# Where the low parts of split weights are subtracted: 45 subtractions move from GpSimd to VectorE

## The chip, the cores and the metric

The kernel runs on one core of a Trainium2 chip. The metric is the device time of one execution in microseconds, as the median of several runs. Beside it stands one execution that was recorded by the hardware profiler, with its own time.

## The reference

Three layers follow each other on a batch of 4 sequences of 576 tokens. All matrix products are wanted at the accuracy of float32.

```python
# attention, 8 heads of 64, over a window of 64 earlier keys
attn = softmax(where(mask, q @ k.T / 8, -1e9)) ; x = attn @ v        # (4, 576, 512)
# gated layer with a spatial product over the tokens
h = relu(x @ w_in)                                                   # 512 -> 1024
u, vv = h[..., :512], h[..., 512:]
vn = (vv - mean) / sqrt(var + 1e-6)
x = (u * (w_spatial @ vn + b_spatial)) @ w_out                       # 512 -> 512
# mixer
u = x + (relu(x.T @ w_tok1) @ w_tok2).T                              # 576 -> 256 -> 576
out = u + relu(u @ w_ch1) @ w_ch2                                    # 512 -> 1536 -> 512
```

The weights come as 64-bit floats; w_tok1 and w_tok2 are called the token weights here, w_ch1 and w_ch2 the channel weights.

## The kernel before

Every product outside the attention is made of three matmuls in a 32-bit format with fewer digits (float32r): an operand x is split into a high part hi, which is x rounded to that format, and a low part lo = x - hi; `mm3` then adds up hi*hi, hi*lo and lo*hi in PSUM. So each operand needs a cast (on ScalarE) and a subtraction (on VectorE or GpSimd) before TensorE can use it.

The work comes in stages. Until about 255 us the kernel does the attention, in 18 iterations, with the first products of the gated layer between them (`uv_u`, `uv_v`) and its product over the tokens (`spatial`); w_in, w_spatial and w_out are loaded by `load_split`. None of that is touched. The order on TensorE and on the DMA queue of SP is written out by hand in the iterations; after them, and on the other engines throughout, a planner, which simulates the instructions with costs of its own, puts each engine's instructions in order when the kernel is built. Each engine then runs its own queue strictly in that order.

After the iterations come, in the order of the program text:

- The token weights: five calls of `load_wide` (tiles t_h and t_l), through the pool lw.
- `wout(b)` for each of four batches: the gated product U (line 386) is split into gh and gl, four pieces of 128x576 each, in five buffers for gh and five for gl; then four by two groups of 12 matmuls, whose results ScalarE copies back into U (line 396).
- `x2nat(b)`: transposes of U on TensorE (line 407), and the split of the result into nh and nl (line 257). `tok1(b)` and `tok2(b)` are the two token products; tok1 splits its result into hh and hl (line 420), tok2 adds to U (line 431).
- The channel weights: w_ch1 in twelve blocks c1 (c1h, c1l) and w_ch2 in twelve blocks c2 (c2h, c2l), each one call of `load_wide` of 128x512. Blocks c1 0 to 3 are loaded beside wout; the pool p3 for the next ones opens when wout is done, and the pool c2p, for c2 3 to 11 and c1 7 to 11, opens when tok2(3) is done, since it takes the room of earlier tiles.
- The channel products over six chunks of 384 tokens: `ch1` (into the tile mm) gives g3h (line 486) and g3l (line 487, VectorE), and `ch2` (line 497, into the tile A) adds up over twelve blocks. In the first chunk of tokens the blocks are still being loaded.

One call of `load_wide` handles one chunk of a weight: a DMA into wraw (three buffers), ScalarE's absolute value into wval (line 106, two buffers), four VectorE instructions that build the 32-bit float (lines 107, 109, 110 and 111), ScalarE's cast to the high part (line 112), and the subtraction for the low part (line 113), which also frees the buffer of wval for the chunk after next. In the rows "wval" is the 32-bit float, and each line number names the same step.

In `spatial`, VectorE adds the bias to a product in PSUM (line 301, tile tmp) and multiplies U by it (line 302); three PSUM tiles of the pool psmm go round among all the mm products, so TensorE waits when line 301 is late.

Of the kernel before, what the change touches and what calls it, by code (L numbers as in the profile page):

```python
# [13 lines left out]
ALU = mybir.AluOpType  # L14
# [13 lines left out]
def f(ap):  # L28
    return ap.bitcast(F32)
# [3 lines left out]
def tile_kernel(ctx, tc, qT, kT, kE, v, w_in, wsT, b_sp, w_out, w_t1, w_t2, w_c1, w_c2, mask, outT):  # L33

    nc = tc.nc
# [57 lines left out]
    def load_wide(pl, hi, lo, src, rows=P, dup=False, wmax=S):  # L93

        shape = list(src.shape[1:])
        n = shape[0] * (shape[1] if len(shape) > 1 else 1)
        raw = pl.tile([P, 2 * wmax], F32, tag="wraw", name="wraw", bufs=3).bitcast(I32)[:, :2 * n]
        val = pl.tile([P, wmax], F32, tag="wval", name="wval", bufs=2)
        for r0 in (0, 64) if dup else (0,):
            dst = raw[r0:r0 + rows]  # L100
            nc.sync.dma_start(out=dst.rearrange("p (a c) -> p a c", a=shape[0]) if len(shape) > 1 else dst, in_=src.bitcast(I32))
        tot = P if dup else rows
        r3 = raw.rearrange("p (n w) -> p n w", w=2)
        low, high = r3[:tot, :, 0], r3[:tot, :, 1]
        x = val[:tot, :n]
        nc.scalar.activation(out=x, in_=f(high), func=AF.Abs)
        nc.vector.tensor_scalar(out=x, in0=x, scalar1=TINY, scalar2=None, op0=ALU.max)  # L107
        xi = x.bitcast(I32)
        nc.vector.tensor_scalar(out=xi, in0=xi, scalar1=0x07FFFFFF, scalar2=3, op0=ALU.bitwise_and, op1=ALU.logical_shift_left)  # L109
        nc.vector.scalar_tensor_tensor(out=xi, in0=high, scalar=-0x40000000, in1=xi, op0=ALU.bitwise_and, op1=ALU.bitwise_or)  # L110
        nc.vector.scalar_tensor_tensor(out=xi, in0=low, scalar=29, in1=xi, op0=ALU.logical_shift_right, op1=ALU.bitwise_or)  # L111
        nc.scalar.copy(out=hi, in_=x)  # L112
        nc.gpsimd.tensor_tensor(out=lo, in0=x, in1=f(hi), op=ALU.subtract)  # L113

    def mm3(o, steps, tail=()):

        todo = []
        for sh, sl, mh, ml in steps:
            todo += [(sh, mh), (sh, ml), (sl, mh)]
        todo += tail  # L120
        n = len(todo)
        for i, (a, c) in enumerate(todo):
            nc.tensor.matmul(o, a, c, start=(i == 0), stop=(i == n - 1))  # L123
# [250 lines left out]
    for k in (0, 2):  # L374
        load_wide(lw, t1_h[:, k:k + 2, :].rearrange("p k c -> p (k c)"), t1_l[:, k:k + 2, :].rearrange("p k c -> p (k c)"),
                  w_t1[128 * k:128 * k + 256, :].rearrange("(k p) c -> p k c", p=P))
    load_wide(lw, t1_h[:, 4, :], t1_l[:, 4, :], w_t1[512:, :], rows=64, dup=True)
    for k in range(2):
        load_wide(lw, t2_h[:, k, :], t2_l[:, k, :], w_t2[128 * k:128 * k + 128, :])

    def wout(b):
        gt = []
        for d in range(4):
            gh = gp.tile([P, S], F32R, tag="gh", name="gh", bufs=5)
            gl = gp.tile([P, S], F32R, tag="gl", name="gl", bufs=5)
            us = U[:, d, b * S:b * S + S]
            nc.scalar.copy(out=gh, in_=us)
            nc.gpsimd.tensor_tensor(out=gl, in0=us, in1=f(gh), op=ALU.subtract)  # L388
            gt.append((gh, gl))
        for d in range(4):  # L390
            dc = slice(128 * d, 128 * d + 128)
            for c0 in (0, 288):
                cs = slice(c0, c0 + 288)
                ps = psmm.tile([P, 512], F32, tag="mm", name="mm")
                mm3(ps[:, :288], [(wo_h[:, k, dc], wo_l[:, k, dc], gt[k][0][:, cs], gt[k][1][:, cs]) for k in range(4)])
                nc.scalar.copy(out=U[:, d, b * S + c0:b * S + c0 + 288], in_=ps[:, :288])
# [45 lines left out]
    def load_c2(pl, k):  # L442
        c2[k] = [pl.tile([P, DM], F32R, name=f"c2{x}{k}") for x in "hl"]
        load_wide(lw, *c2[k], w_c2[128 * k:128 * k + 128, :], wmax=wmax)

    wout(0)
    run_work(len(work))
    ws_stack.close()
    c1p = pool("c1p", "left", stack=c_stack, bufs=1)
    hp = pool("hp", "left", stack=c_stack, bufs=1)  # L450
    x2nat(0)
    wout(1)
    tok1(0)
    load_c1(c1p, 0)
    x2nat(1)
    wout(2)
    tok2(0)
    load_c1(c1p, 1)
# [135 lines left out]
```

## Time and profile before

| what | value |
|---|---|
| median of 3 runs | 702.94 us (702.53 to 703.41) |
| the profiled execution | 704.92 us |
| its span in the profile | 703.1 us |
| busy: TensorE, VectorE, ScalarE, GpSimd | 657.1, 347.8, 252.6, 129.6 us |
| granted clock of TensorE, mean | 0.982 |

In what follows PE is TensorE (PEld its weight loads), DVE is VectorE, ACT is ScalarE, POOL is GpSimd and SP the engine that issues the DMAs. A busy share is an average over stages. A matmul's end is modelled, so that a PE that is shown as busy is not always at its full pace. The names "out<-in" are the program's tiles.

### The profile page before, as it was taken

How to read it: one execution, taken by the hardware profiler on the slowest of the kernel's cores; microseconds unless marked ns; L12 is line 12 of the kernel's file. 1: busy time of each engine (PE TensorE's matmuls, PEld its weight loads, DVE VectorE, ACT ScalarE, POOL GpSimd, SP SyncE). 2: the span in 40 equal slices, each digit the busy share in tenths (PEclk: the TensorE clock that was granted, in tenths of full speed). 3: DMA queues.
4: the chain of work that ended last, by engine and by line, in shares of the span. 5: the costliest groups of instructions: out<-in, count | busy, mean ns of one | idle time of the engine just before them, and what ended most of it. 6: DMA issues, size and time to landing. Idle time of an engine off the chain costs nothing.

```text
span 703.1 us, 11915 instructions
## 1 busy us (share of the span) xinstructions
PE 657.1 (93%) x4744; PEld 627.7 (89%) x4744; DVE 347.8 (49%) x912; ACT 252.6 (36%) x675; POOL 129.6 (18%) x134
## 2 busy tenths in 40 slices
PE   2398899999999998899999998999999999999997
PEld 2387799899989898799998996999999999999996
DVE  4977576645574589921369689701311312212112
ACT  3667672553664353642345154301211111111110
POOL 2534410101220173632012143300000000000000
PEclk8589999999999999999999999999999999999999
DMA  8626552322240034100042234100100100100001
GB/s 287 199 78 186 182 170 69 116 90 68 84 151 2 1 104 129 60 1 1 1 150 91 89 121 150 45 1 1 46 1 0 46 1 1 46 0 13 34 1 45
DMA packets 27286, 50.24 MB, mean 71 GB/s; under 512 B 2784, under 2 KB 13408, under 8 KB 27232
## 3 DMA queue, kind: packets, MB, share of 16 engines
q1 hardware_dynamic: 27232, 49.49, 22.2%
q8 instruction: 37, 0.61, 0.4%
q14 instruction: 17, 0.14, 0.1%
HBM read 44.76 MB, written 4.72 MB: 70 GB/s over the span
## 4 chain that ended last, share of the span: by engine, by line
PE 75%; DVE 11%; DMA 6%; ACT 3%; issue 2%; POOL 1%; SPq 1%; DVEq 0%; POOLq 0%; ACTq 0%
PE mm L123 44%; PE A L497 20%; PE sc L184 3%; DVE wval L110 3%; PE A L123 3%; DMA kk<-in_kT 2%; PE xo L225 2%; DVE wval L111 2%; PE pt L213 2%; ACT pb L199 2%; DVE wval L107 1%; DMA raw<-in_wsT 1%; DMA U<-in_w_in 1%; DVE wval L109 1%; SPq L157 1%
## 5 line engine op out<-in xcount | busy, mean ns | idle before, releaser
L487 DVE SCALAR_TENSOR_TENSOR g3l<-mm,g3h 128x384 fp32r<-128x384 f32 x72 | 40.0, 557 | 191.0 <-ACT g3h L486 191.0
L486 ACT ACTIVATE g3h<-mm 128x384 fp32r<-128x384 f32 x72 | 35.3, 493 | 220.2 <-PE mm L123 220.1
L123 PE MATMUL mm<-uh,c1h 128*128 128x384 f32 x288 | 97.0, 337 | 1.2 <-ACT c1h L112 1.2
L497 PE MATMUL A<-g3h,c2l 128*128 128x384 f32 x288 | 97.2, 338 | 0.8 <-POOL c2l L113 0.8
L123 PE MATMUL mm<-uh,c1l 128*128 128x384 f32 x288 | 96.8, 337 | 1.2 <-POOL c1l L113 1.2
L123 PE MATMUL mm<-ul,c1h 128*128 128x384 f32 x288 | 96.7, 336 | 0.0
L497 PE MATMUL A<-g3l,c2h 128*128 128x384 f32 x288 | 94.1, 337 | 0.0
L497 PE MATMUL A<-g3h,c2h 128*128 128x384 f32 x288 | 93.7, 338 | 0.0
L199 ACT ACTIVATE pb<-pb,nm 128x128 f32<-128x128 f32 x144 | 55.9, 391 | 16.8 <-DVE nm L197 13.9
L184 PE MATMUL sc<-kk,QZ 128*64 128x128 f32 x576 | 39.7, 297 | 22.5 <-DMA kk<-in_kT 16.3
L184 PEld LDWEIGHTS sc<-kk,QZ 128*64 128x64 f32 x576 | 35.8, 152 | 23.2 <-issue 21.6
L123 PEld LDWEIGHTS mm<-uh,c1h 128*128 128x128 f32 x288 | 54.0, 188 | 1.9 <-ACT c1h L112 1.9
L123 PEld LDWEIGHTS mm<-uh,c1l 128*128 128x128 f32 x288 | 54.0, 188 | 1.9 <-POOL c1l L113 1.9
L497 PEld LDWEIGHTS A<-g3h,c2l 128*128 128x128 f32 x288 | 54.0, 187 | 1.5 <-POOL c2l L113 1.4
L497 PEld LDWEIGHTS A<-g3h,c2h 128*128 128x128 f32 x288 | 53.6, 187 | 0.6 <-ACT c2h L112 0.5
L123 PEld LDWEIGHTS mm<-ul,c1h 128*128 128x128 f32 x288 | 54.0, 188 | 0.0
L497 PEld LDWEIGHTS A<-g3l,c2h 128*128 128x128 f32 x288 | 53.8, 188 | 0.0
L123 PE MATMUL mm<-ws_h,nh 128*128 128x288 f32 x160 | 47.3, 300 | 1.9 <-DVE tmp L301 1.7
L123 PE MATMUL mm<-ws_l,nh 128*128 128x288 f32 x160 | 46.5, 295 | 0.0
L123 PE MATMUL mm<-gh,wo_h 128*128 128x288 f32 x128 | 38.2, 301 | 1.0 <-DVE tmp L301 0.8
L123 PE MATMUL mm<-gl,wo_h 128*128 128x288 f32 x128 | 38.1, 298 | 0.6 <-POOL gl L388 0.4
L194 DVE CUSTOM_DVE_ANT_0 pb<-sc,msk 128x128 f32<-128x128 f32 x144 | 33.4, 283 | 9.3 <-PE sc L184 9.3
(111 smaller groups left out, 1433.0 us busy)
## 6 DMA issues: line engine op xcount, KB each, us to landing
wraw<-in_w_c SPq DMA_DIRECT2D x24, 512.0 KB, 3.5
kk<-in_kT SPq DMA_DIRECT2D x16, 384.0 KB, 4.2
QZ<-in_qT SPq DMA_DIRECT2D x36, 128.0 KB, 4.1
va<-in_v SPq DMA_DIRECT2D x18, 256.0 KB, 3.1
vb<-in_v SPq DMA_DIRECT2D x18, 256.0 KB, 4.0
outT<-ot SPq DMA_DIRECT2D x24, 192.0 KB, 2.0
U<-in_w_in SPq DMA_DIRECT2D x8, 512.0 KB, 5.6
raw<-in_w_out SPq DMA_DIRECT2D x8, 256.0 KB, 3.6
```

What stands on the lines that cost most here:

```text
L107: nc.vector.tensor_scalar(out=x, in0=x, scalar1=TINY, scalar2=None, op0=ALU.max)
L110: nc.vector.scalar_tensor_tensor(out=xi, in0=high, scalar=-0x40000000, in1=xi, op0=ALU.bitwise_and, op1=ALU.bitwise_or)
L111: nc.vector.scalar_tensor_tensor(out=xi, in0=low, scalar=29, in1=xi, op0=ALU.logical_shift_right, op1=ALU.bitwise_or)
L123: nc.tensor.matmul(o, a, c, start=(i == 0), stop=(i == n - 1))
L184: nc.tensor.matmul(sc[64 * q:64 * q + 64, h, :], qz[:, h % 2, j, 64 * q:64 * q + 64], kk[:, j, step * q:step * q + 128], start=True, stop= ...
L194: nc.vector.tensor_tensor_reduce(out=half[:, h, :], in0=scs[g][:, h, :], in1=mk, scale=1.0, scalar=-3e38, op0=ALU.add, op1=ALU.max, accum_ ...
L199: nc.scalar.activation(out=half[:, h, :], in_=half[:, h, :], func=AF.Exp, scale=SCALE, bias=nm[:, h:h + 1], accum_out=sm[:, h:h + 1])
L213: nc.tensor.transpose(pt[:, h, :], pb[:, 4 * g + h, :], ident)
L225: nc.tensor.matmul(xo[64 * e:64 * e + 64, j, 64 * q:64 * q + 64], vt[q][:, hc], PT[:, 2 * j + e, 64 * q:64 * q + 64], start=True, stop=True)
L486: nc.scalar.activation(out=gh, in_=ps[:, :CW], func=AF.Relu)
L487: nc.vector.scalar_tensor_tensor(out=gl, in0=ps[:, :CW], scalar=0.0, in1=f(gh), op0=ALU.max, op1=ALU.subtract)
L497: nc.tensor.matmul(acc[d][:, :CW], a, c, start=(ft == 0 and i == 0), stop=(ft == 11 and i == 2))
```

## The change

Two subtractions are issued to VectorE where they were issued to GpSimd: the low part of a chunk in `load_wide`, which serves the token and channel weights, and the low part gl of the gated input in `wout`. The arithmetic is the same. The subtraction in `load_split` (w_in, w_spatial, w_out itself) stays on GpSimd.

```diff
@@ load_wide
         nc.scalar.copy(out=hi, in_=x)
-        nc.gpsimd.tensor_tensor(out=lo, in0=x, in1=f(hi), op=ALU.subtract)
+        nc.vector.tensor_tensor(out=lo, in0=x, in1=f(hi), op=ALU.subtract)
@@ wout
             nc.scalar.copy(out=gh, in_=us)
-            nc.gpsimd.tensor_tensor(out=gl, in0=us, in1=f(gh), op=ALU.subtract)
+            nc.vector.tensor_tensor(out=gl, in0=us, in1=f(gh), op=ALU.subtract)
             gt.append((gh, gl))
```

## Rows read from the trace of the kernel before

**Rows 1.** The page, part 1: busy time, share of the span, instructions of each engine.

```profile
PE 657.1 (93%) x4744; PEld 627.7 (89%) x4744; DVE 347.8 (49%) x912; ACT 252.6 (36%) x675; POOL 129.6 (18%) x134
```

**Rows 2.** Windows: stretch, its length, busy us (instructions) of each engine, granted clock, DMA.

```profile
255.00:285.00 30.00, 27.35 (x200) 26.22 (x199) 28.19 (x43) 12.54 (x24) 16.13 (x12) 1.00 0.43 137
285.00:300.00 15.00, 11.59 (x70) 9.57 (x70) 14.76 (x15) 9.54 (x19) 11.61 (x8) 1.00 0.10 34
300.00:320.00 20.00, 20.00 (x144) 19.30 (x144) 4.60 (x8) 9.27 (x19) 5.78 (x5) 1.00 0.01 1
370.00:390.00 20.00, 18.76 (x111) 17.14 (x110) 19.60 (x34) 8.79 (x17) 5.56 (x4) 1.00 0.33 106
420.00:440.00 20.00, 16.76 (x87) 14.38 (x86) 19.55 (x28) 9.12 (x15) 7.19 (x6) 1.00 0.50 157
465.00:600.00 135.00, 135.00 (x771) 135.00 (x770) 28.60 (x47) 19.83 (x35) 0.00 (x0) 1.00 0.04 14
```

**Rows 3.** Groups of GpSimd: line, operation, tiles, count | busy us, mean ns.

```profile
L388 POOL TENSOR_TENSOR gl<-U,gh 128x576 fp32r<-128x576 f32 x16 | 24.5, 1563 | 20.4 <-ACT gh L387 20.4
...
L113 POOL TENSOR_TENSOR c2l<-wval,c2h 128x512 fp32r<-128x512 f32 x12 | 17.4, 1450 | 36.7 <-ACT c2h L112 36.7
L113 POOL TENSOR_TENSOR c1l<-wval,c1h 128x512 fp32r<-128x512 f32 x12 | 17.0, 1420 | 59.5 <-ACT c1h L112 59.5
...
L113 POOL TENSOR_TENSOR t_l<-wval,t_h 128x512 fp32r<-128x512 f32 (+2 forms) x5 | 7.1, 1419 | 11.8 <-ACT t_h L112 11.8
```

**Rows 4.** Timeline 254 to 266 us: start, duration, engine, line, tiles.

```profile
255.59 7.82 POOL L388 TENSOR_TENSOR gl<-U,gh 128x576 fp32r<-128x576 f32 x5
...
258.87 1.69 DVE L302 TENSOR_TENSOR U<-tmp,U 128x288 f32<-128x288 f32 x1
...
262.06 1.63 DVE L107 TENSOR_SCALAR wval<-wval 128x512 f32<-128x512 f32 x1
...
264.22 0.45 DVE L301 TENSOR_TENSOR tmp<-mm,bb 128x288 f32<-128x288 f32 x1
...
264.72 0.40 PE L123 MATMUL mm<-ws_h,nh 128*128 128x288 f32 x1 [1.72 <-DVE tmp L301]
```

**Rows 5.** Timeline 285 to 298 us.

```profile
287.79 1.74 DVE L110 SCALAR_TENSOR_TENSOR wval<-wraw,wval 128x512 int32<-128x512 int32 x1
...
294.53 1.79 DVE L110 SCALAR_TENSOR_TENSOR wval<-wraw,wval 128x512 int32<-128x512 int32 x1
...
296.24 1.28 DVE L257 TENSOR_TENSOR nl<-A,nh 128x512 fp32r<-128x512 f32 x2
...
296.97 0.50 PE L123 MATMUL A<-nh,t_h 128*128 128x512 f32 x1 [1.65 <-DVE nl L257]
```

**Rows 6.** Timeline 426 to 434 us, two chunks of the last loads.

```profile
426.41 1.28 POOL L113 TENSOR_TENSOR c2l<-wval,c2h 128x512 fp32r<-128x512 f32 x1 [2.00 <-ACT c2h L112]
...
426.51 1.73 DVE L110 SCALAR_TENSOR_TENSOR wval<-wraw,wval 128x512 int32<-128x512 int32 x1
...
428.63 0.68 DVE L111 SCALAR_TENSOR_TENSOR wval<-wraw,wval 128x512 int32<-128x512 int32 x1
429.23 0.41 DVE L107 TENSOR_SCALAR wval<-wval 128x512 f32<-128x512 f32 x1
429.34 0.62 ACT L112 CAST c1h<-wval 128x512 fp32r<-128x512 f32 x1 [0.94 <-DVE wval L111]
...
430.14 1.72 DVE L110 SCALAR_TENSOR_TENSOR wval<-wraw,wval 128x512 int32<-128x512 int32 x1
...
433.42 1.73 DVE L110 SCALAR_TENSOR_TENSOR wval<-wraw,wval 128x512 int32<-128x512 int32 x1
```

**Rows 7.** Groups of VectorE by shape, line 110.

```profile
L110 DVE SCALAR_TENSOR_TENSOR wval<-wraw,wval 128x512 int32<-128x512 int32 x26 | 32.1, 1233 | 0.5
```

**Rows 8.** Instructions of line 257: durations in ns, shortest/median/longest.

```profile
L257 DVE TENSOR_TENSOR nl<-vf,nh x16: 677/686/1157, 64.6 to 252.7; 128x512 fp32r<-128x512 f32 x16
L257 DVE TENSOR_TENSOR nl<-A,nh x16: 675/680/692, 296.2 to 378.6; 128x512 fp32r<-128x512 f32 x16
```

## The prediction

> **What bounds the kernel now.** Begin with the busy times: TensorE is at 93% of the span, VectorE at half [rows 1]. That names TensorE, but an average doesn't say where a microsecond can still be gained, so next come the stretches. From 465 to 600 us TensorE runs 771 matmuls in 135.0 us without a gap, 0.175 us each: no faster VectorE helps there. From 300 to 320 it is full too, with VectorE busy for 4.6 of 20 us. Only four stretches show TensorE idle: 2.65 us in 255 to 285, 3.41 in 285 to 300, 1.24 in 370 to 390, 3.24 in 420 to 440; in all four VectorE is busy 94 to 98% of the time [rows 2]. The idle figures are too small, because the profile models a matmul after a gap as longer. In 420 to 440 there are 87 matmuls, 15.2 us at 0.175, so 4.8 us are lost where 3.24 show. The same factor, 1.48, on the others gives an estimate of 3.9, 5.0, 1.8 and 4.8, in sum 15.5 us. That is all that any relief of VectorE can bring after 255 us; before it no instruction of the change runs.
>
> Why VectorE is late is seen in the timeline. While GpSimd computes five gl in a row (7.82 us from 255.59), VectorE's L302 lasts 1.69 us and its L107 1.63 us (three such pieces in series, the first and the last shown), against 0.41 for an L107 that meets nothing [rows 6] and 0.45 for the like-sized L301 that stands behind them until 264.22; TensorE waits 1.72 us for that one [rows 4]. From 287.79 five VectorE pieces in a row last 1.5 to 1.8 us beside GpSimd's next four gl (the first and the last shown); behind them stands the nl for which TensorE waits 1.65 us [rows 5]. From 426 on every GpSimd subtraction of L113 stretches the L110 that starts beside it to 1.73 us, where L111, the same kind of instruction at the same size, takes 0.68 [rows 6]. So a GpSimd subtraction costs VectorE about 1.05 us when they meet. Over the whole trace the 26 L110 of this size have a mean of 1.233 us [rows 7]: against 0.68 that is 14.4 us of stretching on this one line of the five that are stretched.
>
> **The change, part by part.** It removes from GpSimd 16 gl, 12 c2l, 12 c1l and 5 t_l: 24.5 + 17.4 + 17.0 + 7.1 = 66.0 us [rows 3], so GpSimd should fall from 129.6 to 63.6. VectorE gets 45 instructions. Their form is in the trace: nl<-vf is the same subtraction, two inputs in SBUF, at 128x512, 0.686 us [rows 8]. So 29 of L113 (28 at or near that width) cost 0.69, and 16 of L388 at 576 columns 0.686 x 576/512 = 0.77: 32 us of duration. In a full queue the price is the step from start to start, less than the duration: L111 to the next L107 is 0.60 [rows 6], which makes 0.60 and 0.68, in sum about 28 us. Taken off are the stretched pieces: at least the 14.4 us above, and at most 45 x 1.05 = 47. So VectorE's total hardly moves (I expect 345 to 360 us); what moves is where its time stands, and how long a weight takes.
>
> No instruction of TensorE, ScalarE or SP is added, and no DMA. Two waits change their kind: the sub now waits for ScalarE's cast (L112, L387) in VectorE's queue, and everything behind it there waits too; and the release of wval, for which ScalarE's next L106 waits, comes from VectorE.
>
> *420 to 440 (4.8 us lost).* Here VectorE is the bound: L110 starts at 426.51, 430.14 and 433.42, that is 6.91 us for two chunks and one g3l [rows 6], while TensorE needs 24 matmuls of 0.175 = 4.2 us for the same pair. After the change a pair loses two stretches of 1.05 and gains two subs of 0.60 to 0.69: 6.91 - 2.1 + 1.2 to 1.4 = 6.0 to 6.2. I take 6.0, a gain of 0.9 per pair. Fourteen chunks wait for the pool c2p, which opens when tok2(3) is done; c1 of block 11, the last that TensorE waited for, is the eleventh. That is some five pairs, 4.5 us earlier at the end. Bounds: 1.5 if only the last pairs count, 4.8 if all. I take 4.0.
>
> *285 to 300 (5.0).* VectorE needs 8.45 us from 287.79 to the nl at 296.24 [rows 5]. Unstretched, its L110, L111, L107, L109 and L110 are 0.60 + 0.60 + 0.91 for the two in the middle (429.23 to 430.14 in [rows 6]) + 0.60 = 2.7; four gl and one c1l add 2.7 + 0.6: 6.0, so nl comes 2.4 us earlier and the wait of 1.65 goes; gl itself comes sooner as well. That wait, at 1.48, is 2.4 of the 5.0; the rest I leave. Bounds 0 and 4; I take 2.3.
>
> *255 to 285 (3.9).* Between the L302 at 258.87 and the L301 at 264.22 lie 5.35 us, of which three stretches of 1.2 are 3.6 [rows 4]. What remains is 1.75, and three to five gl go in between, 2.0 to 3.4 us: 3.8 to 5.1, so TensorE's wait shrinks by 0.3 to 1.6. I take 0.9; for the smaller waits of this stretch nothing, since t_l subs come in where stretches go. Bounds 0 and 3.
>
> *370 to 390 (1.8).* Four subs at 0.60 replace at most four stretches of 1.05; half of that 1.8 is met by the longer queue. I take 0.5, bounds -0.5 and 1.5.
>
> *300 to 360.* The remaining seven gl (16 less the five and the four above) are wout(2)'s and wout(3)'s, and cost nothing: VectorE has 15 of 20 us free [rows 2]. Were that cover gone, they would cost 5 us.
>
> Sum: 4.0 + 2.3 + 0.9 + 0.5 = 7.7 us. The profiled execution took 704.92 us with a span of 703.1; it would take 697.2. The runs' median is 702.94, two microseconds below it, so 695.2.
>
> What each stretched row shows is a piece held for most of GpSimd's instruction; nl<-A, whose input lies in PSUM, never exceeds 0.692 us where nl<-vf reaches 1.157 [rows 8]. The Trainium skill's page "SBUF — State Buffer", section "Who interferes with whom", states this as a lock: a VectorE instruction with two SBUF inputs or in a two-port mode, and a GpSimd one that reads SBUF, exclude each other for a whole instruction. By that rule alone each of the 45 GpSimd pieces could hold VectorE for its whole time, 66 us, and with that gone 687.4 us would be left; the sum above goes by the rows, where a piece that meets VectorE costs it 1.05.
>
> **The rivals.**
> *All of it comes back.* The shorter path of a weight (0.69 for 1.3 to 1.45) leaves TensorE no wait that VectorE causes: 15.5 less the 2.6 of the second stretch that no row here gives to VectorE, 690.0. For it: the factor of 6.91 to 6.0. Against it: 6.0 is still above TensorE's 4.2, and VectorE is full in all four stretches.
>
> *It is a trade.* 28 us of subs come for stretching that lies anywhere between 14.4 and 47 us, and TensorE goes on waiting for the same queue: 702 to 703.5. For it: these totals can meet. Against it: the single rows, 1.05 for 0.60. The Trainium skill's page "Perfetto Trace Analysis", section "Identifying the Most-Contended Engine", would have one look at the engine with the highest occupancy first; by it a shift between two engines at 18% and 49% gives nothing, 702.9. The four stretches, where VectorE is the fullest, speak against reading it over the whole span.
>
> *Slower: the sub stands directly behind L111.* The order on VectorE is fixed by a planner. If it puts the sub of a chunk ahead of the next chunk's L107, VectorE idles through ScalarE's cast of 0.62 (429.34 in [rows 6]) and, as I take it, 0.1 of signals. A chunk is then 3.46 - 1.05 + 0.69 + 0.72 = 3.8 against 3.46 now: 0.36 x 11 = 4.0 us more in the last loads; with nothing to 3 us gained before, 704 to 707. It decides once the added idle passes 1.05 - 0.69 = 0.36 us in most chunks. For it: the cast is that long. Against it: another chunk's L107 and L109 (0.9 us) are ready then, since two wval buffers exist.
>
> **How the numbers follow.** No change that a measurement could tell is within 0.2%, 1.4 us: 701.5 to 704.3. Chances: the forecast, 691 to 700, 0.62; all comes back, 687.5 to 691, 0.09; a little, 700 to 701.5, 0.06; a trade 0.09; slower 0.14. Faster is the sum of the first three, 0.77. The range reaches from 688.5 (three quarters of the all-back case) to 702.0, which leaves out the slower case and most of the trade; for the likeliest case alone it is 691 to 700.
>
> **What would show it.** No L110, L107 or L109 after 265 us over 0.8 us; L110's mean at 0.69. GpSimd near 63.6 us and empty after about 257. In the last loads L110 starts every 3.0 us, not 3.46. TensorE's idle time in the stretch of the last loads under 1.5 us. The forecast is wrong if stretched pieces stay without GpSimd beside them, if VectorE shows idle time before subs that wait for ScalarE, or if TensorE waits for a PSUM tile behind a row of gl.

## The result, and the profile after

The changed kernel takes 692.22 us (median of 4 runs, 691.48 to 693.6) against 703.17 for the kernel before (the three runs of the table above and a fourth of 705.62): 10.95 us less by the medians. The ratio of the runs is 0.9838, 95% interval 0.9814 to 0.9861, which makes 11.4 us (9.8 to 13.1). The forecast was 695.2, and 688.5 to 702.0. The profiled execution has a span of 689.9 us. That is 13.2 under the span before, but not all of it is the change: by 255 us, when of the moved subtractions only two gl have started, this execution has done 2160 matmuls, that of the kernel before 2147, and a second one of the changed kernel 2141.

The page's first part after the change (busy us, share, instructions), beside [rows 1]:

```profile
PE 652.9 (95%) x4744; PEld 626.7 (91%) x4744; DVE 345.6 (50%) x957; ACT 252.7 (37%) x675; POOL 64.3 (9%) x89
```

GpSimd has lost 65.3 us and VectorE has gained 45 instructions, yet VectorE's busy time fell by 2.2 us, from 347.8. The groups of VectorE show what it took over and what it got back (compare [rows 3, 7]; the last line has all three sizes of L110 in it):

```profile
L388 DVE TENSOR_TENSOR gl<-U,gh 128x576 fp32r<-128x576 f32 x16 | 11.5, 753 | 13.1 <-ACT gh L387 13.1
...
L113 DVE TENSOR_TENSOR c1l<-wval,c1h 128x512 fp32r<-128x512 f32 x12 | 8.2, 684 | 1.2 <-ACT c1h L112 1.1
L113 DVE TENSOR_TENSOR c2l<-wval,c2h 128x512 fp32r<-128x512 f32 x12 | 8.1, 683 | 0.2 <-ACT c2h L112 0.2
...
L113 DVE TENSOR_TENSOR t_l<-wval,t_h 128x512 fp32r<-128x512 f32 (+2 forms) x5 | 3.3, 655 | 0.0
...
L110 DVE SCALAR_TENSOR_TENSOR wval<-wraw,wval 128x512 int32<-128x512 int32 (+2 forms) x29 | 19.4, 678 | 0.0
```

66.0 us of GpSimd became 31.1 us of VectorE, and L110 has gone from 1.233 us to its unstretched 0.68. The windows say where TensorE got its time back, beside [rows 2]; the stretch 350 to 370 is new:

```profile
255.00:285.00 30.00, 30.00 (x232) 30.00 (x231) 28.39 (x60) 16.44 (x32) 0.00 (x0) 1.00 0.43 139
285.00:300.00 15.00, 15.00 (x97) 14.00 (x96) 11.09 (x19) 9.19 (x19) 0.00 (x0) 1.00 0.01 2
...
350.00:370.00 20.00, 18.63 (x109) 16.53 (x108) 17.59 (x33) 10.57 (x18) 0.00 (x0) 1.00 0.31 106
370.00:390.00 20.00, 19.84 (x128) 19.02 (x127) 15.22 (x33) 4.26 (x8) 0.00 (x0) 1.00 0.33 106
420.00:440.00 20.00, 19.35 (x109) 18.62 (x108) 15.66 (x28) 8.75 (x14) 0.00 (x0) 1.00 0.20 63
465.00:600.00 135.00, 135.00 (x772) 135.00 (x771) 28.91 (x47) 19.83 (x35) 0.00 (x0) 1.00 0.05 18
```

From 255 to 300 TensorE is never idle, where it was for 6.06 us; it does 329 matmuls there in place of 270. In the last loads, the loads of the channel weights from about 402 us on, 0.65 of 20 us are idle in place of 3.24. The full stretch from 465 to 600 is as it was. Of the 1.24 us that were idle in 370 to 390, 0.16 are left, but around 360 us a loss of 1.37 us has come in.

The timeline of the changed kernel, 254 to 264 us, against [rows 4]:

```profile
255.12 0.44 DVE L301 TENSOR_TENSOR tmp<-mm,bb 128x288 f32<-128x288 f32 x1
255.48 1.41 DVE L388 TENSOR_TENSOR gl<-U,gh 128x576 fp32r<-128x576 f32 x2
...
257.19 0.74 DVE L388 TENSOR_TENSOR gl<-U,gh 128x576 fp32r<-128x576 f32 x1
...
257.86 0.44 DVE L301 TENSOR_TENSOR tmp<-mm,bb 128x288 f32<-128x288 f32 x1
```

gl stands one or two at a time between the L301 that empty PSUM. Two of them take 1.41 us together, and TensorE waits for no L301. Before, one stretched piece took as long or longer (1.69 and 1.63 us in [rows 4]).

The last loads, against [rows 6]:

```profile
418.43 0.68 DVE L113 TENSOR_TENSOR c1l<-wval,c1h 128x512 fp32r<-128x512 f32 x1
419.03 0.68 DVE L110 SCALAR_TENSOR_TENSOR wval<-wraw,wval 128x512 int32<-128x512 int32 x1
...
419.75 0.69 DVE L111 SCALAR_TENSOR_TENSOR wval<-wraw,wval 128x512 int32<-128x512 int32 x1
...
420.36 0.42 DVE L107 TENSOR_SCALAR wval<-wval 128x512 f32<-128x512 f32 x1
...
420.81 0.43 DVE L109 TENSOR_SCALAR wval<-wval 128x512 int32<-128x512 int32 x1
...
421.15 0.69 DVE L113 TENSOR_TENSOR c2l<-wval,c2h 128x512 fp32r<-128x512 f32 x1
421.75 0.68 DVE L110 SCALAR_TENSOR_TENSOR wval<-wraw,wval 128x512 int32<-128x512 int32 x1
...
424.21 0.69 DVE L113 TENSOR_TENSOR c1l<-wval,c1h 128x512 fp32r<-128x512 f32 x1
424.82 0.69 DVE L110 SCALAR_TENSOR_TENSOR wval<-wraw,wval 128x512 int32<-128x512 int32 x1
```

From 419.03 to 424.82 two chunks and one g3l take 5.79 us, against 6.91. Each sub (the subtraction of L113) stands after the next chunk's L107 and L109, not directly behind its own L111.

### The profile page after: what moved, and what is told of

The parts are those of the page before. It is cut to its first block, busy times and chain, and to the rows that moved or that the text cites. A ratio compares the mean times of both kernels' runs of the same rounds, so it can differ in the third digit from the quotient of the medians.

```text
span 689.9 us, 11901 instructions
## 1 busy us (share of the span) xinstructions
PE 652.9 (95%) x4744; PEld 626.7 (91%) x4744; DVE 345.6 (50%) x957; ACT 252.7 (37%) x675; POOL 64.3 (9%) x89
## 4 chain that ended last, share of the span: by engine, by line
PE 82%; DMA 6%; DVE 6%; ACT 2%; SPq 2%; issue 1%; POOL 0%; DVEq 0%; ACTq 0%; POOLq 0%
PE mm L123 51%; PE A L497 21%; PE sc L184 4%; DMA kk<-in_kT 3%; DMA wraw<-in_w_c 2%; PE xo L225 2%; PE A L123 2%; PE pt L213 2%; ACT pb L199 1%; PE A L407 1%; DMA U<-in_w_in 1%; SPq L157 1%; DVE wval L110 1%; DVE wval L111 1%; DVE val L79 0%
## 5 line engine op out<-in xcount | busy, mean ns | idle before, releaser
L199 ACT ACTIVATE pb<-pb,nm 128x128 f32<-128x128 f32 x144 | 55.9, 391 | 16.0 <-DVE nm L197 13.1
L123 PE MATMUL mm<-gh,wo_l 128*128 128x288 f32 x128 | 37.8, 296 | 0.0
```

The costliest lines, as they stand in the source:

```text
L199: nc.scalar.activation(out=half[:, h, :], in_=half[:, h, :], func=AF.Exp, scale=SCALE, bias=nm[:, h:h + 1], accum_out=sm[:, h:h + 1])
```

## The experiments

TensorE's idle time in the three stretches that matter is the measure beside the time: the length of the window less TensorE's busy time in it, in us, in one profiled execution of each kernel (with the weights also on GpSimd its slowest, 703.21). Some expectations reckon a loss by the matmuls that are missing in a window instead, which gives larger figures. Each kernel ran beside the kernel before on the same chip, on one of several, so the ratio is the figure to compare.

| kernel | median us | ratio (95%) | 255 to 320 | 354 to 402 | 402 to 465 |
|---|---|---|---|---|---|
| before | 703.17 | 1 | 6.05 | 1.24 | 3.24 |
| changed | 692.22 | 0.9838 (0.9814 to 0.9861) | 0 | 1.53 | 1.09 |
| changed, again | 692.79 | 0.9827 (0.9803 to 0.9852) | 0 | 0.52 | 1.09 |
| only gl moved | 698.15 | 0.9910 (0.9890 to 0.9930) | 1.80 | 0.96 | 3.24 |
| only weights moved | 696.16 | 0.9886 (0.9866 to 0.9906) | 3.57 | 0.70 | 1.09 |
| changed, weights also on GpSimd | 700.61 | 0.9950 (0.9933 to 0.9966) | 0.65 | 1.03 | 5.41 |
| changed, gl also on GpSimd | 700.98 | 0.9952 (0.9933 to 0.9971) | 5.30 | 0.87 | 1.08 |
| changed, weights twice on VectorE | 698.75 | 0.9935 (0.9911 to 0.9958) | 0 | 0.05 | 7.34 |
| changed, three wval | 692.90 | 0.9827 (0.9800 to 0.9853) | 1.76 | 0.07 | 0.64 |
| before, three wval | 706.70 | 1.0041 (1.0019 to 1.0063) | 6.41 | 2.86 | 1.60 |
| all three on VectorE | 690.01 | 0.9810 (0.9778 to 0.9842) | 0 | 0 | 1.06 |
| all three, again | 688.85 | 0.9785 (0.9758 to 0.9811) | 0 | 0 | 1.09 |
| all three, three wval | 691.62 | 0.9809 (0.9784 to 0.9833) | 1.56 | 0.02 | 0 |

The theory was that the gain is the end of the stretching: VectorE's pieces are held while GpSimd subtracts. Its rivals were a shorter path of each weight to TensorE, and a better order from the planner, which plans anew when an instruction changes its engine.

**One half alone.** First only gl, then only the weights:

```diff
@@ only gl: wout
-            nc.gpsimd.tensor_tensor(out=gl, in0=us, in1=f(gh), op=ALU.subtract)
+            nc.vector.tensor_tensor(out=gl, in0=us, in1=f(gh), op=ALU.subtract)
@@ only the weights: load_wide
-        nc.gpsimd.tensor_tensor(out=lo, in0=x, in1=f(hi), op=ALU.subtract)
+        nc.vector.tensor_tensor(out=lo, in0=x, in1=f(hi), op=ALU.subtract)
```

> Only the gl of wout are moved to VectorE; the 29 subtractions of the weights stay on GpSimd. If the gain is the end of the stretching (a VectorE piece held while GpSimd subtracts): TensorE's idle time in 255 to 300 falls from 6.1 us to 1 to 3, since 9 GpSimd pieces of weights remain there, and the last loads stay as before (3.2 us idle in about 20 us, an L110 every 3.4 us); time 696 to 699 us. If the gain is the shorter path of a weight to TensorE: gl is on no such path, the gain is under 2 us, 701 to 703 us.

> Only the 29 subtractions of the weights are moved; the 16 gl stay on GpSimd. End of the stretching: in the last loads an L110 every 3.0 us and TensorE idle for 1 us or less in place of 3.2; in 255 to 300 the nine gl still hold VectorE (pieces of 1.5 us and more, TensorE idle for 3 us or more); time 697 to 700 us, and its gain and that of the gl alone add up to the 11 us of the whole change. If the planner's new order is what counts, the two gains need not add up, and the sum may be off by 4 us or more to either side.

Each half takes away the idle time of its own stretch: gl alone 4.25 of the 6.05 us and nothing of the last loads, which keep their 3.24 us; the weights alone the whole gain of the last loads, 3.24 to 1.09, and 2.5 of the 6.05. The time of the second, 696.16, lies a little under the expected 697 to 700. The two gains add up to 2.0% against 1.6%, a little more than the whole, within their intervals; in the first stretch both halves stretch VectorE, and either one relieves it. That speaks against the path of a weight as the main cause in the first stretch, since gl is on no such path, but each half also has an order of its own, so this leaves the planner open.

**The stretching back, the order kept.** This is the experiment that decides. Every subtraction stays on VectorE, and GpSimd computes one of the same shape beside it, whose result nobody reads (GpSimd's copy of it, below):

```diff
@@ weights: load_wide
         nc.vector.tensor_tensor(out=lo, in0=x, in1=f(hi), op=ALU.subtract)
+        scr = pl.tile([P, wmax], F32, tag="scr", name="scr", bufs=1)
+        nc.gpsimd.tensor_tensor(out=scr[:tot, :n], in0=f(hi), in1=f(hi), op=ALU.subtract)
@@ gl, in the other kernel: wout
             nc.vector.tensor_tensor(out=gl, in0=us, in1=f(gh), op=ALU.subtract)
+            scr = lw.tile([P, S], F32, tag="scr", name="scr", bufs=1)
+            nc.gpsimd.tensor_tensor(out=scr, in0=f(gh), in1=f(gh), op=ALU.subtract)
```

In both kernels the queues of TensorE, VectorE and ScalarE hold the instructions of the changed kernel in the same order, row for row, in the traces too (4744, 957 and 675 rows).

> The whole change, and in addition GpSimd computes a subtraction of the same shape for each of the 29 weight chunks, hi - hi into a scratch tile that nobody reads. It needs the cast only, and nothing waits for it; the order of the instructions on TensorE, VectorE and ScalarE is that of the changed kernel, row for row. If the stretching is the cause: pieces of 1.5 to 1.8 us are back on VectorE beside GpSimd's, the mean of L110 rises from 0.69 to over 1.0, a pair of chunks takes up to 8 us in place of 6, and the time is 700 to 708 us, so that the whole gain on the weights is lost though all subs are on VectorE. If the planner's order or the shorter path of a weight made the gain: 692 us, within 1.

> The whole change, and in addition GpSimd computes gh - gh, at gl's shape, into a scratch tile that nobody reads, for each of the 16 gl. The order on TensorE, VectorE and ScalarE is that of the changed kernel, row for row. If the first stretches were won by the end of the stretching: pieces of 1.5 us and more come back on VectorE in 255 to 300, TensorE loses 3 to 7 us there in place of none, the last loads keep their 2.3 us, and the time is 695 to 699 us. If they were won by the planner's new order: no loss in 255 to 300, 692 us within 1.

Both give most of the gain back: 700.61 and 700.98 us, some 8 of the 11.4 us each by the ratios; the second is above the 695 to 699 that were expected. Between 255 and 465 us TensorE does 1272 matmuls in the kernel before, 1331 and 1342 in the two executions of the changed one, and 1295 and 1291 with the copies. The loss comes back where the GpSimd pieces are and nowhere else: with the weights copied 5.41 us in the last loads (more than the 3.24 of before, since VectorE now has the subs and the stretching), with gl copied 5.30 us in 255 to 320. The window of the latter:

```profile
255.00:320.00 65.00, 59.70 (x417) 57.11 (x416) 56.33 (x86) 31.76 (x63) 20.26 (x14) 0.97 0.23 71
```

Its timelines of VectorE, GpSimd and TensorE:

```profile
257.77 0.45 DVE L301 TENSOR_TENSOR tmp<-mm,bb 128x288 f32<-128x288 f32 x1
258.14 2.95 DVE L388 TENSOR_TENSOR gl<-U,gh 128x576 fp32r<-128x576 f32 x2
261.01 1.39 DVE L302 TENSOR_TENSOR U<-tmp,U 128x288 f32<-128x288 f32 x1
262.33 1.70 DVE L388 TENSOR_TENSOR gl<-U,gh 128x576 fp32r<-128x576 f32 x1
263.95 0.45 DVE L301 TENSOR_TENSOR tmp<-mm,bb 128x288 f32<-128x288 f32 x1
...
255.57 7.85 POOL L388 TENSOR_TENSOR scr<-gh 128x576 f32<-128x576 f32 x5
...
264.45 0.40 PE L123 MATMUL mm<-ws_h,nh 128*128 128x288 f32 x1 [3.33 <-DVE tmp L301]
```

The two gl that took 1.41 us take 2.95, the L302 takes 1.39, and the L301 for which TensorE waits starts at 263.95. With the weights copied the timelines of VectorE and GpSimd in the last loads read:

```profile
424.48 1.53 DVE L110 SCALAR_TENSOR_TENSOR wval<-wraw,wval 128x512 int32<-128x512 int32 x1
...
428.39 1.53 DVE L110 SCALAR_TENSOR_TENSOR wval<-wraw,wval 128x512 int32<-128x512 int32 x1
...
431.96 1.53 DVE L110 SCALAR_TENSOR_TENSOR wval<-wraw,wval 128x512 int32<-128x512 int32 x1
...
427.87 1.51 POOL L113 TENSOR_TENSOR scr<-c1h 128x512 f32<-128x512 f32 x1 [2.41 <-ACT c1h L112]
```

A pair takes 431.96 - 424.48 = 7.48 us, against 5.79; the mean of all 29 L110 is 0.944 us against 0.678. The expectation of over 1.0 for that mean was a little high: some copies meet other pieces, or none. With order and path of the changed kernel, most of its gain is lost by GpSimd's pieces alone.

Not all of that loss is idle time. Behind TensorE's waits in these stretches its granted clock falls, where it stays at 1.00 from 255 to 465 us in the kernel before and the changed one: with the weights copied TensorE is idle for 1.07 and 1.32 us up to 421.54, and runs 423 to 424 at half, the lower of its two levels, 1.2 GHz. Windows of that kernel:

```profile
420.00:440.00 20.00, 15.66 (x75) 14.06 (x74) 19.76 (x31) 7.70 (x13) 8.04 (x6) 0.91 0.41 131
...
423.00:424.00 1.00, 1.00 (x5) 1.00 (x4) 0.97 (x4) 0.62 (x1) 0.04 (x1) 0.50 0.00 0
```

A mean of 0.91 over 20 us is 1.8 us of full pace lost (an estimate); with gl copied it is 0.97 over 65 us, about as much.

One thing the copies don't separate. In the last loads of the kernel before, 2.0 of the 3.24 us that TensorE was idle ended with GpSimd's own subtraction, as here:

```profile
431.36 0.44 PE L123 MATMUL mm<-uh,c1l 128*128 128x384 f32 x1 [0.74 <-POOL c1l L113]
```

On VectorE that subtraction takes 0.68 us in place of 1.28, and what this shorter last step is worth by itself no run shows.

**The price of a sub in VectorE's own queue.** The scratch subtraction of the weights, on VectorE:

```diff
-        nc.gpsimd.tensor_tensor(out=scr[:tot, :n], in0=f(hi), in1=f(hi), op=ALU.subtract)
+        nc.vector.tensor_tensor(out=scr[:tot, :n], in0=f(hi), in1=f(hi), op=ALU.subtract)
```

> The changed kernel with the scratch subtraction of the 29 weight chunks on VectorE in place of GpSimd: each weight costs VectorE a second piece of 0.60 from start to start, and nothing is stretched. If one subtraction beside VectorE on GpSimd costs it more than doing it itself: the last loads lose less than with the scratch subtraction on GpSimd (there 8.6 us), a pair of chunks 7.2 us in place of 8.1, and the time is 695 to 699 us against 700.6. If the change is a trade, the two are equal, 700 us and more.

The time, 698.75 us, lies in the range expected, though its interval overlaps that of the copy on GpSimd; and the last loads lose 7.34 us, more than with that copy, where less was expected. This kernel has another order. VectorE's timeline:

```profile
412.67 0.69 DVE L113 TENSOR_TENSOR c1l<-wval,c1h 128x512 fp32r<-128x512 f32 x1
413.28 0.69 DVE L113 TENSOR_TENSOR scr<-c1h 128x512 f32<-128x512 f32 x1
413.88 0.69 DVE L113 TENSOR_TENSOR c2l<-wval,c2h 128x512 fp32r<-128x512 f32 x1
414.49 0.68 DVE L113 TENSOR_TENSOR scr<-c2h 128x512 f32<-128x512 f32 x1
...
416.49 0.43 DVE L107 TENSOR_SCALAR wval<-wval 128x512 f32<-128x512 f32 x1 [0.98 <-ACT wval L106]
```

The planner puts the four subs of a pair in a row, behind both L111; the second wval comes free late, and VectorE then idles 0.98 us for ScalarE's L106. That is akin to the slower rival of the prediction, but not the same: VectorE waits for a wval that came free late, not through the cast. The steps themselves are 0.60 to 0.61 (412.67, 413.28, 413.88), as assumed, but the run can't say what a sub costs in an order like that of the changed kernel.

**The path of a weight.** A third buffer for wval, in the changed kernel and in the kernel before:

```diff
-        val = pl.tile([P, wmax], F32, tag="wval", name="wval", bufs=2)
+        val = pl.tile([P, wmax], F32, tag="wval", name="wval", bufs=3)
```

> The changed kernel with three buffers for wval in place of two. If what is still lost in the last loads (some 2.3 us) is the wait of ScalarE's absolute value for a free wval, which the sub now frees from VectorE's queue: the loss goes, 689.5 to 690.5 us. If VectorE's own time per chunk is the bound there: 691.5 to 693 us, and L110 still starts every 3.0 us.

> The kernel before, subtractions on GpSimd, with three wval buffers in place of two: the release of wval by GpSimd's 1.3 us no longer holds ScalarE back. If the shorter path of a weight is a part of the gain: the last loads lose 2 us or less in place of 5.2, 698 to 701 us. If the stretched VectorE pieces bound them: L110 still starts every 3.4 us, the loss there is over 4 us, 702 to 704 us.

In the changed kernel the last loads lose 0.64 us in place of 1.09, but 255 to 320 loses 1.76 us in place of none, and the time is the same: 692.9. No piece of VectorE is stretched there; TensorE's waits in its timeline are all for ScalarE's copies:

```profile
284.88 0.44 PE L407 MATMUL A<-ident,U 128*128 128x128 f32 x2 [0.46 <-ACT U L396]
286.89 0.55 PE L407 MATMUL A<-ident,U 128*128 128x128 f32 x3 [0.92 <-ACT U L396]
291.52 0.40 PE L123 MATMUL mm<-gh,wo_h 128*128 128x288 f32 x1 [0.39 <-ACT U L396]
```

So the planner's order can cost up to 1.8 us of idle time in that stretch. In the kernel before, the last loads fall to 1.60 us idle, as the path theory has it, but 2.86 us are lost in 354 to 402, and the time is 706.7, above both expectations and 0.4% slower than before. The three idle times sum to 10.87 us, hardly more than the 10.53 before; but behind a wait of 2.12 us the granted clock falls here too, to a mean of 0.92 over 380 to 402, some 1.8 us of full pace (an estimate). The loss moves to an earlier load; a longer reach of ScalarE doesn't take the place of VectorE's time.

**The third subtraction too.** Both kernels leave the one of load_split on GpSimd:

```diff
-        nc.gpsimd.tensor_tensor(out=lo[:tot], in0=val[:tot, :n], in1=f(hi[:tot]), op=ALU.subtract)
+        nc.vector.tensor_tensor(out=lo[:tot], in0=val[:tot, :n], in1=f(hi[:tot]), op=ALU.subtract)
```

> The changed kernel with the third subtraction, that of load_split (w_in, w_spatial, w_out: 26 pieces), on VectorE too. The stretched pieces before 255 us (some 15 us of stretching in the changed kernel, half of it in the first 40 us) shrink. If they hold TensorE up there: the first 90 us get 1 to 4 us shorter, 688 to 691 us. If TensorE waits there for transfers and ScalarE: 692 us within 1.5, by the planner's order to either side.

> The changed kernel once more, as the measure for the two runs beside it: 692.2 us within 1, a ratio to the kernel before of 0.982 to 0.986.

> All three subtractions on VectorE, once more beside the changed kernel. In its first profile the first 90 us were no shorter, but the 2.8 us that the changed kernel loses in 354 to 402 were gone. If that is the planner's order and repeats with each execution: 2 to 3 us under the changed kernel, 689 to 690.5 us. If its first 690.0 us were chance: within 1 us of the changed kernel.

> All three subtractions on VectorE and three wval buffers. With three buffers alone the last loads lost 1.1 us in place of 2.3, but 255 to 320 lost 2.9 us in place of none, by another order. If the third buffer helps the last loads whatever the order: 1 us under the kernel with all subtractions on VectorE where no new loss comes in, 688.5 to 690 us. If the planner's order decides: anything from 688.5 to 693 us.

Its medians are the lowest of all: 690.01 us, and 688.85 beside 692.79 for the changed kernel on the same chip, a ratio of 0.9785 against 0.9827. The intervals still meet at their edges, so that it is faster than the changed kernel is likely and not shown. The first 255 us, where these subtractions run, are hardly shorter: it has done 2162 and 2163 matmuls by then, the changed kernel 2160 and 2141. So its lower time doesn't come from where it was expected. In both its profiles the stretch 354 to 402 has no idle TensorE. That stretch turned out to be no matter of VectorE's pieces alone. The changed kernel's timelines of ScalarE, VectorE and TensorE in its first profile:

```profile
357.11 0.67 ACT L106 ACTIVATE wval<-wraw 128x512 f32<-128x512 f32 x1 [2.72 <-DMA wraw<-in_w_c]
...
357.81 0.43 DVE L107 TENSOR_SCALAR wval<-wval 128x512 f32<-128x512 f32 x1 [2.30 <-ACT wval L106]
...
362.80 0.66 PE L407 MATMUL A<-ident,U 128*128 128x128 f32 x4 [0.82 <-DVE hl L420]
```

ScalarE waits 2.72 us for the transfer of a weight, VectorE stands idle for 2.30 us, and the hl for which TensorE waits comes late. In the second profile of the same kernel ScalarE waited 1.25 us for that transfer, and TensorE lost 0.52 us in place of 1.53; with all subtractions on VectorE the wait was 0.74 us in one profile and none in the other. Why the transfer lands sooner there was not tried. The third buffer added to it gives 691.62: the last loads lose nothing, but the order loses 1.56 us in 255 to 320 again.

## Why the prediction was right, and where its sizes were off

**The total.** The mechanism was right and its size too small: 7.7 us forecast, 11.4 measured. 692.2 lies inside the range, but nearer to the rival "all of it comes back" (690.0) than to the forecast of 695.2, and two terms missed in opposite directions: the last loads by 1.4 us too much, 255 to 300 by some 5 too little. That the total came as near as it did is in part luck.

**The place.** That time can come back only in the four stretches, and there because VectorE is full, held: the matmul rate from 465 to 600 is unchanged, and the estimate of 15.5 us lost was above the gain of 11.4, as it had to be.

**The mechanism.** Stretched pieces were expected to vanish and did. Told as the signs that were named ahead: L110's mean 0.68 against 0.69, GpSimd 64.3 us against 63.6, VectorE's total 345.6 in 345 to 360, a pair of chunks 5.79 us against 6.0, TensorE's idle time in the last loads 1.09 against under 1.5. One sign of being wrong did show: VectorE idles before subs that wait for ScalarE's cast, 13.1 us before gl alone (the row of L388 above); but TensorE, busy without a gap from 255 to 350, waits for none of it. That the stretching is the cause and not the order was only argued in the prediction; the two kernels with GpSimd's copies show that the stretching is enough for most of the loss. The section "Who interferes with whom" of the Trainium skill's page "SBUF — State Buffer" has a VectorE instruction with two SBUF inputs contend with a GpSimd one that reads SBUF. The trace agrees: beside a GpSimd subtraction that nobody waits for, VectorE's L110 takes 1.53 us in place of 0.68, and L302 and gl are stretched likewise, while L301, with one input in PSUM, stays at 0.45 (257.77, beside the scr from 255.57 on).

**The last loads.** Predicted 4.0 us; measured, by the same count of matmuls at 0.175 us in 402 to 465, 334 before (4.5 us lost of 63) and 349 after (1.9 lost): 2.6. The pair was as fast as assumed, but the gain of 0.9 was counted for five pairs. In the kernel before the first L110 of these loads, up to 416.17, are not stretched; the first piece that is longer by about 1 us is the L111 at 416.88, and TensorE's last wait ends at 436.92. The timelines of VectorE and TensorE there:

```profile
416.17 0.68 DVE L110 SCALAR_TENSOR_TENSOR wval<-wraw,wval 128x512 int32<-128x512 int32 x1
416.88 1.66 DVE L111 SCALAR_TENSOR_TENSOR wval<-wraw,wval 128x512 int32<-128x512 int32 x1
...
436.92 0.44 PE L123 MATMUL mm<-uh,c1h 128*128 128x384 f32 x1 [0.61 <-ACT c1h L112]
```

Six such pieces lie between (416.88, 419.67, 423.57, 426.51, 430.14, 433.42), three pairs and not five; 3 x 0.9 = 2.7 (an estimate).

**255 to 300.** Here the size was wrong: 3.2 us predicted, nearly all of the 8.9 came back. Two terms failed. One is "three to five gl go in between": it put the new gl ahead of the L301 that TensorE waits for, while the planner set them between the L301, where they cost nothing. The other is the 2.6 us that no row gave to VectorE and that were left standing. They were waits for ScalarE, 0.91 and 0.25 us, and for GpSimd's own gl, 0.37 us; TensorE's timeline of the kernel before has

```profile
289.68 0.55 PE L407 MATMUL A<-ident,U 128*128 128x128 f32 x3 [0.91 <-ACT U L396]
...
292.69 0.40 PE L123 MATMUL mm<-gl,wo_h 128*128 128x288 f32 x1 [0.37 <-POOL gl L388]
```

The changed kernel has none of them; that with the third buffer waits for ScalarE's U again. With gl copied on GpSimd, in the same order, 5.30 us of idle time come back where 6.05 were, so the stretching is enough for most of it; what part the order has isn't shown.

**370 to 390.** Predicted 0.5 us of gain. The loss moved to about 360, where a transfer that ScalarE waits for sets it: from 354 to 402 TensorE idles 1.53 us in one execution of the changed kernel and 0.52 in the other, against 1.24 before. So the sign isn't settled, at a size that hardly counts.

**The rivals.** A trade, 702 us or more, is excluded; it took the totals, which are indeed almost equal, for the answer. So is the reading by the Trainium skill's page "Perfetto Trace Analysis", section "Identifying the Most-Contended Engine", over the whole span, which would have given 702.9: two engines at 18% and 49% held up the one at 93%. In the last loads of the changed kernel the sub doesn't stand directly behind its L111, so the slower rival didn't come about; with the weights twice on VectorE something akin did. That all comes back, 690.0, or 687.4 with all of the 15.5 us, fell short by the last loads and the stretch at 360.

## What to carry to other kernels

A second engine is no free hand when its instruction makes the first one's longer: look for one line whose durations fall into two groups, and see what the neighbour does during the long ones. Compare such prices piece by piece in the stretch where the bound engine waits; totals over the span are blind to it. To tell a contention from a new instruction order, put the contending instruction back as a copy that nobody reads, and see that the queues of the other engines stay the same.

## What the runs showed of the hardware that was not expected

The holding goes both ways. In the kernel before, a GpSimd subtraction that takes 1.29 us takes 2.79 when a long VectorE subtraction has started just ahead of it; its timelines of GpSimd and VectorE:

```profile
443.53 1.29 POOL L113 TENSOR_TENSOR c2l<-wval,c2h 128x512 fp32r<-128x512 f32 x1 [2.01 <-ACT c2h L112]
447.06 2.79 POOL L113 TENSOR_TENSOR c2l<-wval,c2h 128x512 fp32r<-128x512 f32 x1 [2.23 <-ACT c2h L112]
...
446.95 1.75 DVE L477 TENSOR_TENSOR ul<-U,uh 128x1536 fp32r<-128x1536 f32 x1
```

And it holds instructions with one tensor input as well, when that lies in SBUF: L107, 0.41 us, took 1.63 [rows 4, 6].

What a meeting costs follows from when GpSimd is through. In [rows 6] GpSimd's subtraction ends at 427.69 and the L110 beside it at 428.24, 0.55 us later; with the weights copied the two end at 429.38 and 429.92, 0.54 later. In both most of the 0.68 us that an L110 takes lie behind GpSimd's end, as if it had begun only then: in these rows the price of a meeting is what is left of GpSimd's instruction when VectorE's turn comes, here some 0.85 to 1.05 us.
